# Zero-weight matmuls added into the open attention output bank while the planned recent TensorE use is low

## The chip, the cores and the metric

One core of one Trainium2 chip runs the whole program. The metric is the device time of one execution in microseconds (us); lower is better. The kernel before has a median of 971.56 us over 3 runs (968.69 to 973.88).

## The reference, cut to what matters

A pre-norm transformer block on 2048 rows of 640 numbers in bf16: attention with 32 heads of 20 columns, no mask, then a gated MLP of width 1728, each added to its input.

```python
def _A_ref(x, wqkv, wo):
    H = 32; Dh = D // H
    qkv = (x @ wqkv).reshape(B, S, 3, H, Dh)...
    scores = jnp.einsum("bhqd,bhkd->bhqk", q, k) * (Dh ** -0.5)
    p = _softmax(scores, axis=-1)
    o = jnp.einsum("bhqk,bhkd->bhqd", p, v)
    return o... @ wo
def _B_ref(x, w_gate, w_up, w_down):
    h = _gelu(x @ w_gate) * (x @ w_up)
    return h @ w_down
h = x + _A_ref(_layernorm(x), A_wqkv, A_wo)
h2 = h + _B_ref(_layernorm(h), B_w_gate, B_w_up, B_w_down)
```

The 32 x 2048 x 2048 exponentials of the softmax are the largest single item of work.

## The kernel before, in words

**Stages.** The first 40 us or so load x and the weights, do the first layer norm and project the first keys and queries. Then comes attention, in 7 chunks of queries (`CHUNKS`: 512, 512, 256, 256, 256, 128, 128). A chunk is cut into slots of 512 output columns (32 slots in all), a slot into 64 tiles of 128 keys x 512 score columns. What follows attention for a chunk (output projection, second layer norm, MLP: `post`, line 938) runs in the background of the next chunk's attention; for the last chunk it is the tail of the kernel.

**A unit of attention** (`unit`, line 787) is 3 tiles, then 2, in turn: banks 0 to 2 of PSUM and banks 3 and 4. TensorE writes the scores (`qk_mms`, line 804; recorded at L808) as up to 4 matmuls beside each other in row strips of 32. ScalarE takes the exponential of the whole unit in one instruction into a ring of 18 tiles (`pts` and `pts2`, which lies in `rege`). Some 8 tiles of a slot get their exponential on VectorE instead (`d_exp`, line 759, L768 and after), from a bank of the background (7 or 5). When two rows of 4 tiles ("quads") are done, one planned operation multiplies them with V (line 885): 4 matmuls of a quad beside each other in column strips of 32, accumulated in bank 6, 32 rows of it for each of 4 heads. It is called PV here; the ring's places come free when the whole operation has ended, since the semaphore goes with its last matmul. After a slot's last PV (`final`) VectorE copies bank 6 out (`osb`, line 904), and `epilogue` (line 899) transposes and divides; the next slot's first PV waits for that copy.

**The order of the work** is not left to the engines. Each operation is handed to a planner (`Sched.op`, line 52) with its engine, a duration, a priority (`P_QK` 0, `P_PV` 1, `P_EPI` 2, `P_BG` 3), what it reads and writes, the banks it takes, and `util`, the array time that it counts for. `Sched.schedule` (line 83) simulates the engines and, whenever one is free, gives it the ready operation of the best priority; on TensorE it prefers, below the first priority, an operation of the same mode (row strips, column strips, full array). `emit` (line 204) writes each engine's list in that order, with semaphore waits. An operation, once started, isn't interrupted.

**The filler that is there already** (lines 157 to 172): where TensorE is free in the plan and nothing is ready, and bank 7 has no owner, and the planned `util` of the last 3.4 us (`WARM_WIN`) is under half of that (`WARM_MIN`), a full 128x128 by 512 matmul of K data into bank 7 (`sc.warm`, line 1051) is planned, 0.215 us long. Nobody reads its result.

Of the kernel before, what the change touches and what calls it, by code (L numbers as in the profile page):

```python
# [15 lines left out]
SEM_ANY = 0.036  # L16
DRAIN = {"pe": 0.165, "act": 0.115, "dve": 0.085, "pool": 0.05, "sp": 0.0}
WARM_WIN, WARM_MIN = 3.4, 0.5
PE_AGE = 1.5

MODE_SWITCH = {"pe": 0.105, "act": 1.28}
# [19 lines left out]
class Sched:  # L41
# [3 lines left out]
    def __init__(self, nc):  # L45
        self.nc = nc
        self.ops = []
        self.lw = {}
        self.rd = {}
        self.warm = None  # L50

    def op(self, eng, fns, dur, prio, reads=(), writes=(), acq=(), rel=(), after=(), sem=None, lat=None, mode=None, util=0.0):
        o = Op()
# [29 lines left out]
    def schedule(self):  # L83
        ops = self.ops
        for o in ops:
            o.nd = len(o.deps)
            for d in o.deps:
                ops[d].succ.append(o.i)
        free_at = [0.0] * 8
        owner = [None] * 8  # L90
        last = [None] * 8
        ready = {e: [] for e in ENGINES}
        future = {e: [] for e in ENGINES}
        free = {e: 0.0 for e in ENGINES}
        mode = {e: None for e in ENGINES}
        for o in ops:
            if o.nd == 0:
                heapq.heappush(ready[o.eng], (o.prio, o.i))
        events = [0.0]
        done = 0  # L100
        order = []
        t = 0.0
        recent = collections.deque()
        total = len(ops)
        while done < total:
            assert events, "no operation can start"
            t = heapq.heappop(events)
            while events and events[0] <= t + 1e-9:
                heapq.heappop(events)
            for e in ENGINES:  # L110
                while future[e] and future[e][0][0] <= t + 1e-9:
                    _, p, i = heapq.heappop(future[e])
                    heapq.heappush(ready[e], (p, i))
                if free[e] > t + 1e-9:
                    continue
                skipped = []
                kept = set()
                chosen = None
                while ready[e]:
                    p, i = heapq.heappop(ready[e])  # L120
                    o = ops[i]
                    got = []
                    for bk in o.acq:
                        for b in bk.allowed:
                            if owner[b] is None and free_at[b] <= t + 1e-9 and b not in got and b not in kept:
                                got.append(b)
                                break
                        else:
                            got = None
                            break  # L130
                    if got is None:

                        if p[0] == 0:
                            kept.update(bk.allowed[0] for bk in o.acq)
                        skipped.append((p, i))
                        continue
                    skipped.append((p, i))
                    if chosen is None:
                        chosen, banks = o, got
                        if e != "pe" or p[0] < 1 or o.mode == mode[e] or t - o.ready > PE_AGE:  # L140
                            break
                    elif o.mode == mode[e]:
                        chosen, banks = o, got
                        break
                    if len(skipped) >= 60:
                        break
                for s in skipped:
                    if chosen is None or s[1] != chosen.i:
                        heapq.heappush(ready[e], s)
                if chosen is not None:  # L150
                    for bk, b in zip(chosen.acq, banks):
                        bk.b = b
                        owner[b] = bk
                        if last[b] is not None:
                            chosen.deps = set(chosen.deps)
                            chosen.deps.add(last[b])
                if chosen is None:
                    if e == "pe" and self.warm is not None:
                        while recent and recent[0][0] < t - WARM_WIN:
                            recent.popleft()  # L160
                        b = self.warm_bank
                        if owner[b] is None and free_at[b] <= t + 1e-9 and sum(x for _, x in recent) < WARM_MIN * WARM_WIN:
                            o = Op()
                            o.i, o.eng, o.fns, o.dur, o.lat = len(ops), "pe", [self.warm], 0.215, DRAIN["pe"]
                            o.prio, o.sem, o.tag, o.mode, o.util = (9, 0), None, "warm", "full", 0.213
                            o.deps = set(self.warm_deps) | ({last[b]} if last[b] is not None else set())
                            o.acq, o.rel, o.succ = [], [], []
                            if all(hasattr(ops[d], "fin") and ops[d].fin + 0.06 <= t for d in self.warm_deps):
                                ops.append(o)
                                last[b] = o.i  # L170
                                chosen = o
                                total += 1
                    if chosen is None:
                        continue
                o = chosen
                o.start = t
                if o.util:
                    recent.append((t, o.util))
                if o.mode is not None:
                    if mode[e] not in (None, o.mode):  # L180
                        o.dur += MODE_SWITCH[e]
                    mode[e] = o.mode
                free[e] = t + o.dur
                o.fin = t + o.dur + o.lat
                heapq.heappush(events, free[e])
                for bk in o.rel:
                    b = bk.b
                    owner[b] = None
                    free_at[b] = o.fin + SEM_LAT.get((e, "pe"), SEM_ANY)
                    last[b] = o.i  # L190
                    heapq.heappush(events, free_at[b])
                for s in o.succ:
                    q = ops[s]
                    q.ready = max(q.ready, free[e] if q.eng == e == "pe" else o.fin + SEM_LAT.get((e, q.eng), SEM_ANY))
                    q.nd -= 1
                    if q.nd == 0:
                        heapq.heappush(future[q.eng], (q.ready, q.prio, q.i))
                        heapq.heappush(events, q.ready)
                order.append(o)
                done += 1  # L200
        self.order = order
        self.span = max(o.fin for o in ops)
# [93 lines left out]
P_QK, P_PV, P_EPI, P_BG = 0, 1, 2, 3  # L296


def bass_sequential_preLN__mha_block__glu_gated_geglu__prompt_kernel(
# [12 lines left out]
    with ExitStack() as es:  # L312
        sc = Sched(nc)
        op = sc.op

        def sb(name, shape, dt=BF16):
            return es.enter_context(nc.sbuf_tensor(name, shape, dt))
# [15 lines left out]
        ident = sb("ident", [128, 128])  # L333
        identf = sb("identf", [128, 128], FP32)
        sel = sb("sel", [128, NA, H])
        sel0 = sb("sel0", [128, 4, 32])
        off0 = sb("off0", [128, 1], FP32)
        stats = sb("stats", [128, 4, 2, 6], FP32)
# [88 lines left out]
        def cst(fn, key, n=128):  # L427
            op(POOL, fn, 0.1 + n * 0.001, P_BG, writes=[key, "pool"])
# [6 lines left out]
        def fills(g0, g1, c0, c1):  # L435
# [3 lines left out]
            for c in range(c0, c1):  # L439
# [6 lines left out]
        cst(I("affine_select", out=sel[:], in_=sel[:], compare_op=ALU.is_ge, fill=0.0, base=DH - 1,  # L446
              pattern=[[-128, NA], [DH, H]], channel_multiplier=-1), "sel", 160)
        cst(I("memset", sel0[:], 0.0), "sel0")
        cst(I("memset", off0[:], 0.0), "off0", 1)
        for j in range(4):  # L450
            cst(I("memset", off0[32 * j:32 * j + 1, :], OFF), "off0", 1)
# [335 lines left out]
        def unit(u):  # L787
# [52 lines left out]
            while pv_wait:  # L840
# [35 lines left out]
                    acq = [bk]  # L876
                else:
                    bk, acq = pv_bank[s_], []
                fns, reads = [], ["vones"]
                for have in quads:  # L880
                    for kk in range(nk):
                        for pt, pkey, (_, g, kb, j) in have:
# [4 lines left out]
                                         tile_position=(0, 32 * j), skip_group_check=True))  # L887
                            pv_open.add((s_, j))
                            reads += [pkey, ("v", kt, g // 4)]
                op("pe", fns, 0.218 * len(quads), P_PV, mode="col", util=0.213 * len(quads), reads=reads, writes=[("O", s_), "pvseq"], acq=acq)  # L890
                if final:
                    assert not d_done and not d_raw
                    epilogue(s_, bk)

# [43 lines left out]
        def post(c, banks, tail):  # L938
# [88 lines left out]
            for tt in range(tb, tb + nt):  # L1027
                t = q0 // 128 + tt - tb
                i = t % 2
                for hf in range(2):  # L1030
# [19 lines left out]
        q_bound0(PRO, P_EPI)  # L1050
        sc.warm = I("matmul", PS[:, 512 * 7:512 * 8], kt_all[:, 0, 0:128], kt_all[:, 0, 0:512], start=True, stop=True,
                    skip_group_check=True)
        sc.warm_bank = 7
        sc.warm_deps = tuple(sc.lw[kk] for kk in k_keys[0][0])
        for kt in range(NT):
# [69 lines left out]
```

## Time and profile before

| | |
|---|---|
| median of 3 runs | 971.56 us |
| the profiled execution's own time | 969.62 us |
| its span, first to last instruction | 967.9 us |
| mean granted TensorE clock | 0.965 |
| ScalarE busy | 884.8 us (91%) |
| TensorE busy | 861.9 us (89%) |
| VectorE busy | 830.8 us (86%) |

A busy time is the union of the records of an engine's instructions. The end of a matmul is modelled, and records of consecutive instructions of one engine overlap, since an instruction begins while the one before it drains; so a busy engine need not be at its peak, and a wait shows shorter as idle time than it delays the next start.

### The profile page before, as it was taken

The page shows a single profiled execution, that of the slowest core. Times are in us where ns is not written, and L with a number is a line of the kernel's source. Part 1 is how long each engine was busy: PE and PEld are TensorE (multiplying, and loading weights), DVE is VectorE, ACT ScalarE, POOL GpSimd, SP SyncE. Part 2 cuts the span into 40 slices and gives each one's busy share as a digit, 9 for nine tenths or more (in the row PEclk, how much of TensorE's full clock was granted, in tenths as well). Part 3 has the DMA queues.
Part 4 walks back from the last instruction along what each step waited for, and adds up shares of the span by engine and source line. Part 5 has one row for each costly group of instructions (what it writes and reads, how often), then busy time and mean ns, then how long its engine had stood idle before and what let it go on. Part 6 is the DMA issues. An engine that isn't in the chain of part 4 may idle for free.

```text
span 967.9 us, 22233 instructions
## 1 busy us (share of the span) xinstructions
PE 861.9 (89%) x9668; PEld 366.4 (38%) x9668; DVE 830.8 (86%) x1804; ACT 884.8 (91%) x789; POOL 17.8 (2%) x25
## 2 busy tenths in 40 slices
PE   3999899998788899998888998999889999998998
PEld 1432222222132223233243333344334445655577
DVE  8758988998799898987899998798989899889953
ACT  4798999989999999999999999999989999998931
POOL 7000000000000000000000000000000000000000
PEclk9996998999999999999999899999979999998999
DMA  6220203227100000001000000001000000000000
GB/s 244 68 63 25 62 8 85 69 74 263 42 1 2 1 1 1 1 15 41 1 2 2 2 1 1 1 9 29 22 1 1 2 28 3 2 24 2 3 22 15
DMA packets 22041, 30.04 MB, mean 31 GB/s; under 512 B 1964, under 2 KB 19464, under 8 KB 21944
## 3 DMA queue, kind: packets, MB, share of 16 engines
q1 hardware_dynamic: 21944, 28.63, 9.2%
q8 instruction: 75, 1.23, 0.6%
q14 instruction: 22, 0.18, 0.1%
HBM read 20.12 MB, written 8.09 MB: 29 GB/s over the span
## 4 chain that ended last, share of the span: by engine, by line
ACT 70%; PE 20%; DVE 8%; issue 0%; DMA 0%; DVEq 0%
ACT pts L320 44%; ACT rege L320 24%; PE ps L808 5%; PE ps L571 4%; PE ps L320 4%; PE ps L984 3%; PE ps L1035 3%; DVE rege L320 3%; DVE rege L768 1%; ACT L320 1%; DVE qt_all L320 1%; PE ps L535 1%; DVE stats L320 1%; DMA rege<-in_A_x_dram 0%; DVE regw L601 0%
## 5 line engine op out<-in xcount | busy, mean ns | idle before, releaser
L320 ACT ACTIVATE pts<-ps 128x1536 bf16<-128x1536 f32 x480 | 569.9, 1338 | 26.5 <-PE ps L808 16.3
L808 PE MATMUL ps<-qt_all,kt_all 32*128 32x256 bf16 (+2 forms) x3584 | 315.0, 296 | 61.0 <-ACT pts L320 36.8
L320 ACT ACTIVATE rege<-ps 128x1536 bf16<-128x1536 f32 x239 | 295.6, 1339 | 6.1 <-PE ps L808 4.2
L808 PEld LDWEIGHTS ps<-qt_all,kt_all 32*128 32x128 bf16 x3584 | 98.3, 93 | 293.7 <-ACT pts L320 158.8
L320 DVE TENSOR_TENSOR qt_all<-qt_all 128x1024 bf16<-128x1024 bf16 (+1 forms) x240 | 164.7, 686 | 2.8
L984 PE MATMUL ps<-rege,regw 128*128 128x256 bf16 (+2 forms) x980 | 152.9, 292 | 6.3 <-ACT rege L320 2.5
L320 PE MATMUL ps<-pts,v_all 128*21 128x256 bf16 (+2 forms) x2098 | 144.9, 299 | 0.0
L768 DVE TENSOR_SCALAR rege<-ps 128x512 int16<-128x512 f32 x154 | 105.7, 687 | 43.8 <-PE ps L808 43.0
L320 PE MATMUL ps<-rege,v_all 128*21 128x256 bf16 (+2 forms) x1294 | 118.0, 301 | 0.5 <-DVE rege L320 0.5
L320 DVE TENSOR_SCALAR qt_all<-qt_all 128x1024 bf16<-128x1024 int16 (+1 forms) x288 | 116.0, 419 | 1.7
L984 PEld LDWEIGHTS ps<-rege,regw 128*128 128x128 bf16 x980 | 74.0, 98 | 61.5 <-issue 21.3
L571 PE MATMUL ps<-regw 128*128 128x320 bf16 (+1 forms) x360 | 88.9, 361 | 4.7 <-DVE rege L768 2.1
L1035 PE MATMUL ps<-regw,rege 128*128 128x320 bf16 x448 | 79.0, 304 | 2.3 <-DVE rege L1024 0.8
L768 DVE TENSOR_SCALAR qt_all<-ps 128x512 int16<-128x512 f32 x96 | 65.8, 687 | 5.0 <-PE ps L808 4.2
L320 DVE TENSOR_SCALAR rege<-rege 128x1024 int16<-128x1024 int16 (+2 forms) x166 | 67.8, 424 | 1.1
L320 DVE TENSOR_TENSOR rege<-rege 128x1024 bf16<-128x1024 bf16 (+3 forms) x103 | 66.3, 647 | 1.2
L320 PEld LDWEIGHTS ps<-pts,v_all 128*21 128x21 bf16 x2098 | 51.3, 92 | 39.6 <-issue 33.3
L320 PE MATMUL ps<-kt_all 128*128 128x512 bf16 x160 | 48.4, 395 | 6.8 <-DVE rege L768 5.2
L1035 PEld LDWEIGHTS ps<-regw,rege 128*128 128x128 bf16 x448 | 37.7, 98 | 33.5 <-issue 15.6
L320 PEld LDWEIGHTS ps<-rege,v_all 128*21 128x21 bf16 x1294 | 41.9, 93 | 21.9 <-issue 15.3
L571 PEld LDWEIGHTS ps<-regw 128*128 128x128 bf16 x360 | 29.3, 100 | 49.8 <-issue 19.6
L1024 DVE TENSOR_TENSOR rege<-rege,ps 128x512 bf16<-128x512 bf16 (+1 forms) x53 | 36.0, 680 | 14.0 <-PE ps L984 13.9
(83 smaller groups left out, 593.8 us busy)
## 6 DMA issues: line engine op xcount, KB each, us to landing
rege<-in_A_x_dram SPq DMA_DIRECT2D x6, 640.0 KB, 4.9
q_rows<-regw SPq DMA_DIRECT2D x20, 128.0 KB, 1.7
out_dram<-rege SPq DMA_DIRECT2D x16, 160.0 KB, 1.8
regw<-in_B_w_gate_dram SPq DMA_DIRECT2D x1, 2160.0 KB, 8.0
regw<-in_B_w_up_dram SPq DMA_DIRECT2D x1, 2160.0 KB, 14.0
regw<-in_B_w_down_dram SPq DMA_DIRECT2D x1, 2080.0 KB, 18.7
kt_all<-k_rows SPq DMA_DIRECT2D x12, 160.0 KB
qt_all<-q_rows SPq DMA_DIRECT2D x12, 160.0 KB
```

Source lines behind the costliest of these rows:

```text
L320: return lambda eng: getattr(eng, method)(*args, **kwargs)
L535: op("pe", lambda eng, a=a: eng.transpose(bank16(bk, D)[:, 128 * a:128 * a + 128], src[:, a * 128:(a + 1) * 128], ident[:]), 0.055, prio, ...
L571: yield op("pe", lambda eng, l=l, r=r, k=k: eng.matmul(bank(bk, n), l, r, start=(k == 0), stop=(k == len(steps) - 1)), c_mm(n), prio, mode ...
L768: d_ops.append(op("dve", lambda eng: eng.tensor_scalar(v[:, 512 * h:512 * h + 512], bank(b), EXP_MUL, -32000.0, ALU.mult, ALU.max), c_dve( ...
L808: return lambda eng: eng.matmul(out()[:, kk * nq:(kk + 1) * nq], kt_all[32 * j:32 * j + 32, g, kt * 128:(kt + 1) * 128], qt_all[32 * j:32 ...
L984: op("pe", lambda eng, a=a, f=f, fi=fi: eng.matmul(bank(bk)[:, fi * nq:(fi + 1) * nq], w[:, a, F0[f]:F0[f] + 128], hnT[:, a, 128 * tb:128 ...
L1024: hdone.append(op("dve", lambda eng, bu=bu, fv=fv, w=w: eng.tensor_tensor(fv, fv, bank(bu, w), ALU.mult), c_dve(w), p, reads=[ku, ("ha", k ...
L1035: op("pe", lambda eng, f=f, o=o, hf=hf, bk=bk: eng.matmul(bank(bk, 320), ha_f[:, o:o + 128], wd[:, f, hf * 320:(hf + 1) * 320], start=(f = ...
```

## The change

The planner keeps `live`: true from a PV that isn't its slot's last to the slot's last PV, so while bank 6 holds an open sum. There are two new places for filler, both made of a "pad": 4 matmuls in column strips of 32, with weights of zeros (`zer`, 128x32) and 512 columns of K, which add 0 to all of bank 6 (`start=False`).

- Where TensorE is free in the plan and the planned recent use is under the old limit, filler no longer needs bank 7: while `live`, a pad is planned when bank 7 is taken or the array is in column mode; otherwise the old matmul, as before.
- A PV that finds the planned use of the last 3.4 us, its own counted, under 0.42 of that gets pads inside its own operation, 0.215 us each, until the limit is reached or its own `util` is at least 1.1 (from 0.426 for two quads, so up to 4). Its semaphore then goes with the last pad.

Besides, one memset on GpSimd for `zer`, and two more things that a PV's reads are checked against.

```diff
--- before.py
+++ after.py
@@ -16,6 +16,7 @@
 SEM_ANY = 0.036
 DRAIN = {"pe": 0.165, "act": 0.115, "dve": 0.085, "pool": 0.05, "sp": 0.0}
 WARM_WIN, WARM_MIN = 3.4, 0.5
+PAD_WIN, PAD_MIN = 3.4, 0.42
 PE_AGE = 1.5
 
 MODE_SWITCH = {"pe": 0.105, "act": 1.28}
@@ -48,6 +49,8 @@
         self.lw = {}
         self.rd = {}
         self.warm = None
+        self.pad = None
+        self.final = set()
 
     def op(self, eng, fns, dur, prio, reads=(), writes=(), acq=(), rel=(), after=(), sem=None, lat=None, mode=None, util=0.0):
         o = Op()
@@ -101,6 +104,7 @@
         order = []
         t = 0.0
         recent = collections.deque()
+        live = False
         total = len(ops)
         while done < total:
             assert events, "no operation can start"
@@ -159,20 +163,35 @@
                         while recent and recent[0][0] < t - WARM_WIN:
                             recent.popleft()
                         b = self.warm_bank
-                        if owner[b] is None and free_at[b] <= t + 1e-9 and sum(x for _, x in recent) < WARM_MIN * WARM_WIN:
+                        free7 = (owner[b] is None and free_at[b] <= t + 1e-9
+                                 and all(hasattr(ops[d], "fin") and ops[d].fin + 0.06 <= t for d in self.warm_deps))
+                        if sum(x for _, x in recent) < WARM_MIN * WARM_WIN and (free7 or live):
                             o = Op()
-                            o.i, o.eng, o.fns, o.dur, o.lat = len(ops), "pe", [self.warm], 0.215, DRAIN["pe"]
-                            o.prio, o.sem, o.tag, o.mode, o.util = (9, 0), None, "warm", "full", 0.213
-                            o.deps = set(self.warm_deps) | ({last[b]} if last[b] is not None else set())
-                            o.acq, o.rel, o.succ = [], [], []
-                            if all(hasattr(ops[d], "fin") and ops[d].fin + 0.06 <= t for d in self.warm_deps):
-                                ops.append(o)
+                            o.i, o.eng, o.lat = len(ops), "pe", DRAIN["pe"]
+                            o.prio, o.sem, o.tag, o.util = (9, 0), None, "warm", 0.213
+                            o.acq, o.rel, o.succ, o.dur = [], [], [], 0.215
+                            if live and (mode[e] == "col" or not free7):
+                                o.fns, o.mode, o.deps = list(self.pad), "col", set()
+                            else:
+                                o.fns, o.mode = [self.warm], "full"
+                                o.deps = set(self.warm_deps) | ({last[b]} if last[b] is not None else set())
                                 last[b] = o.i
-                                chosen = o
-                                total += 1
+                            ops.append(o)
+                            chosen = o
+                            total += 1
                     if chosen is None:
                         continue
                 o = chosen
+                if e == "pe" and self.pad is not None and o.tag and o.tag[0] == "O":
+                    while recent and recent[0][0] < t - PAD_WIN:
+                        recent.popleft()
+                    u = sum(x for _, x in recent) + o.util
+                    while u < PAD_MIN * PAD_WIN and o.util < 1.1:
+                        o.fns = o.fns + self.pad
+                        o.dur += 0.215
+                        o.util += 0.213
+                        u += 0.213
+                    live = o.i not in self.final
                 o.start = t
                 if o.util:
                     recent.append((t, o.util))
@@ -333,6 +352,7 @@
         ident = sb("ident", [128, 128])
         identf = sb("identf", [128, 128], FP32)
         sel = sb("sel", [128, NA, H])
+        zer = sb("zer", [128, 32])
         sel0 = sb("sel0", [128, 4, 32])
         off0 = sb("off0", [128, 1], FP32)
         stats = sb("stats", [128, 4, 2, 6], FP32)
@@ -446,6 +466,7 @@
         cst(I("affine_select", out=sel[:], in_=sel[:], compare_op=ALU.is_ge, fill=0.0, base=DH - 1,
               pattern=[[-128, NA], [DH, H]], channel_multiplier=-1), "sel", 160)
         cst(I("memset", sel0[:], 0.0), "sel0")
+        cst(I("memset", zer[:], 0.0), "zer", 32)
         cst(I("memset", off0[:], 0.0), "off0", 1)
         for j in range(4):
             cst(I("memset", off0[32 * j:32 * j + 1, :], OFF), "off0", 1)
@@ -876,7 +897,7 @@
                     acq = [bk]
                 else:
                     bk, acq = pv_bank[s_], []
-                fns, reads = [], ["vones"]
+                fns, reads = [], ["vones", "zer"] + k_keys[0][0]
                 for have in quads:
                     for kk in range(nk):
                         for pt, pkey, (_, g, kb, j) in have:
@@ -887,8 +908,9 @@
                                          tile_position=(0, 32 * j), skip_group_check=True))
                             pv_open.add((s_, j))
                             reads += [pkey, ("v", kt, g // 4)]
-                op("pe", fns, 0.218 * len(quads), P_PV, mode="col", util=0.213 * len(quads), reads=reads, writes=[("O", s_), "pvseq"], acq=acq)
+                pv = op("pe", fns, 0.218 * len(quads), P_PV, mode="col", util=0.213 * len(quads), reads=reads, writes=[("O", s_), "pvseq"], acq=acq)
                 if final:
+                    sc.final.add(pv)
                     assert not d_done and not d_raw
                     epilogue(s_, bk)
 
@@ -1050,6 +1072,8 @@
         q_bound0(PRO, P_EPI)
         sc.warm = I("matmul", PS[:, 512 * 7:512 * 8], kt_all[:, 0, 0:128], kt_all[:, 0, 0:512], start=True, stop=True,
                     skip_group_check=True)
+        sc.pad = [I("matmul", PS[32 * j:32 * j + 32, 512 * 6:512 * 7], zer[:], kt_all[:, 0, 0:512], start=False, stop=False,
+                    tile_position=(0, 32 * j), skip_group_check=True) for j in range(4)]
         sc.warm_bank = 7
         sc.warm_deps = tuple(sc.lw[kk] for kk in k_keys[0][0])
         for kt in range(NT):
```

## Rows read from the trace of the kernel before

**Rows 1.** The page's first part: busy time of each engine, share, instructions.
```profile
PE 861.9 (89%) x9668; PEld 366.4 (38%) x9668; DVE 830.8 (86%) x1804; ACT 884.8 (91%) x789; POOL 17.8 (2%) x25
```
**Rows 2.** The page's fourth part: the chain that ended last, by engine, by line.
```profile
ACT 70%; PE 20%; DVE 8%; issue 0%; DMA 0%; DVEq 0%
ACT pts L320 44%; ACT rege L320 24%; PE ps L808 5%; PE ps L571 4%; PE ps L320 4%; PE ps L984 3%; PE ps L1035 3%; DVE rege L320 3%; DVE rege L768 1%; ACT L320 1%; DVE qt_all L320 1%; PE ps L535 1%; DVE stats L320 1%; DMA rege<-in_A_x_dram 0%; DVE regw L601 0%
```
**Rows 3.** The page's second part: granted clock in tenths, in 40 equal slices.
```profile
PEclk9996998999999999999999899999979999998999
```
**Rows 4.** Windows of the ten half-clock stretches: length, busy by engine, clock.
```profile
core 0: us, PE busy (x) PEld busy (x) DVE busy (x) ACT busy (x) POOL busy (x), PEclk, DMA share, GB/s
77.20:94.30 17.10, 16.50 (x83) 3.84 (x81) 12.96 (x26) 13.07 (x12) 0.00 (x0) 0.50 0.06 16
...
708.70:718.90 10.20, 9.74 (x84) 4.29 (x84) 8.41 (x20) 7.60 (x7) 0.00 (x0) 0.50 0.01 2
...
821.30:824.70 3.40, 3.13 (x19) 1.75 (x15) 3.40 (x9) 3.39 (x3) 0.00 (x0) 0.50 0.00 0
...
sum 68.30, PE 65.51 PEld 21.81 DVE 56.43 ACT 55.19 POOL 0.00; mean PE 6.55 PEld 2.18 DVE 5.64 ACT 5.52 POOL 0.00
```
**Rows 5.** ScalarE's waits over the whole span: total us, times, longest.
```profile
ACT pts L320 <- PE ps L808: 16.3, 21, 4.1
...
ACT pts L320 <- PE ps L320: 9.7, 7, 2.5
...
ACT rege L320 <- PE ps L808: 4.2, 8, 1.2
ACT rege L320 <- PE ps L320: 1.6, 1, 1.6
```
**Rows 6.** Groups by line and shape: the exponentials of 3 and 2 tiles.
```profile
L320 ACT ACTIVATE pts<-ps 128x1536 bf16<-128x1536 f32 x240 | 371.9, 1549 | 17.7 <-PE ps L808 14.1 <-PE ps L320 3.2
L320 ACT ACTIVATE pts<-ps 128x1024 bf16<-128x1024 f32 x240 | 270.2, 1126 | 8.8 <-PE ps L320 6.5 <-PE ps L808 2.2
```
**Rows 7.** The chain in order of time: start, us, engine, instructions merged.
```profile
463.80 4.52 ACT pts L320 x4
470.58 4.52 ACT pts L320 x4
```
**Rows 8.** Windows of the 3.4 us ahead of each fall of the clock.
```profile
323.00:326.40 3.40, 1.95 (x22) 0.59 (x21) 3.40 (x8) 3.40 (x4) 0.00 (x0) 1.00 0.00 0
538.00:541.40 3.40, 2.54 (x37) 1.10 (x37) 3.40 (x9) 3.40 (x4) 0.00 (x0) 1.00 0.00 0
...
817.90:821.30 3.40, 2.69 (x81) 1.84 (x75) 3.40 (x7) 3.38 (x4) 0.00 (x0) 1.00 0.02 5
...
sum 34.00, PE 22.85 PEld 9.22 DVE 33.78 ACT 33.88 POOL 0.62; mean PE 2.29 PEld 0.92 DVE 3.38 ACT 3.39 POOL 0.06
```
**Rows 9.** The old filler: its group, its count from 230.8 to 326.4, that window.
```profile
L320 PE MATMUL ps<-kt_all 128*128 128x512 bf16 x160 | 48.4, 395 | 6.8 <-DVE rege L768 5.2 <-DVE qt_all L768 1.4
L320 PE MATMUL ps<-kt_all 128*128 128x512 bf16 x53 | 15.9, 387 | 2.2 <-DVE rege L768 2.2
230.80:326.40 95.60, 77.47 (x630) 24.07 (x630) 83.63 (x189) 95.04 (x85) 0.00 (x0) 1.00 0.15 59
```
**Rows 10.** Timeline of TensorE around one PV of two quads, full clock.
```profile
94.89 0.39 PE L320 MATMUL ps<-pts,v_all 128*21 128x512 bf16 x3
...
95.12 0.38 PE L320 MATMUL ps<-pts,v_all 128*21 128x512 bf16 x1
...
95.44 0.58 PE L571 MATMUL ps<-regw 128*128 128x320 bf16 x3
```
**Rows 11.** Timeline around a slot's last PV, a long one.
```profile
694.30 0.29 PE L320 MATMUL ps<-pts,v_all 128*21 128x256 bf16 x3
...
695.28 0.40 PE L808 MATMUL ps<-qt_all,kt_all 32*128 32x256 bf16 x6
695.40 2.36 ACT L320 ACTIVATE pts<-ps 128x1536 bf16<-128x1536 f32 x2 [0.88 <-PE ps L320]
```
**Rows 12.** Timeline of GpSimd: a memset like the new one, and its last work.
```profile
4.08 0.20 POOL L320 MEMSET sel<- 128x128 bf16 x1
...
11.94 7.18 POOL L320 MEMSET qt_all<- 128x1792 f32 x4
```

## The prediction, made before the changed kernel was run

> **What bounds the kernel now.** I read the page's totals first. ScalarE is busy 884.8 us, TensorE 861.9, VectorE 830.8 [rows 1]: three engines near the end of their room, so totals don't settle it. The chain of waits does: 70% of the span runs over ScalarE, 44% and 24% of it in the exponentials into the two parts of the ring, and 20% over TensorE [rows 2]. The chain in order of time shows what a quiet stretch looks like: from 463.80 to 470.58 there are three pairs of exponentials, 6.78 us or 2.26 us a pair [rows 7], with nothing between them. There the time is ScalarE's, and no matmul made faster can help.
>
> So a gain has to come from where ScalarE waits. Its waits for the scores are 16.3 and 4.2 us (29 times); its waits for PV, which has to free a place in the ring, are 9.7 and 1.6 us (8 times) [rows 5]. Next I read the clock. It is full in most slices, with dips to 6, 7 or 8 tenths in single ones [rows 3]. Cut at its changes, there are ten stretches at half clock between 77 and 887 us (of the two levels 2.4 and 1.2 GHz the second), together 68.3 us; ScalarE is busy in 55.19 of them and idle in 13.1 [rows 4]. TensorE is busy 65.51 of the 68.3 there: at half clock it is the bound. That is where the chance lies.
>
> **The size of the chance.** A wait delays the next exponential by more than the idle time shown, as the records overlap: a pair's records last 1549 + 1126 ns [rows 6] but a pair takes 2.26 us [rows 7], so 0.21 us of each lies under the next. I take 20 of the 29 waits for scores to lie in the ten stretches, by their share of the idle time (13.1 of 20.5 us). Lost there: 13.1 + 20 x 0.21 = 17.3 us, or 0.25 us for each us at half clock. It is uneven: the stretch from 77.2 has 4.0 idle of 17.1, that from 821.3 has none [rows 4].
>
> **What precedes a fall, and whether the change reaches it.** In the 3.4 us ahead of the ten falls ScalarE runs through (33.88 of 34.0) but TensorE is busy 22.85 of 34, from 1.95 to 2.69 of 3.4 in the rows shown [rows 8]. So 1.1 us a time is idle, and more of the busy part is drain and narrow score strips. The existing filler could have stood there; it needs bank 7, which epilogues, background chains and VectorE's tiles also hold, and it was used 160 times in all, 53 of these between 230.8 and 326.4 [rows 9], in which the clock never fell until the end. New filler goes into bank 6 and needs no other bank: 1.1 us holds five pads of 0.22. Nine of the ten falls lie well inside an open slot by the order of the work; the one at 159.1 comes just after a slot's end, when `live` is off. I let two falls stay, or new ones come, of 6.8 us each: 13.7 x 0.25 = 3.4 us. Gain: 17.3 - 3.4 = 13.9 us.
>
> **What a pad costs on TensorE.** No row shows a pad, but a PV quad is the same shape but for 21 weight columns instead of 32: two quads start at 94.89 and 95.12 and the next operation at 95.44 [rows 10], so 0.23 us a quad and some 0.3 with the change of mode. I take 0.22 to 0.23 us a pad; the ends are 0.21 (512 columns at 2.4 GHz) and 0.33.
>
> Here a rule of the Trainium skill speaks against the change ("TensorE: Matmul & The Clock Gate", the section Part 3 on packing small matmuls): weight loads run beside matmuls in flight only when their row group differs, and a pad's four loads use all rows. With that page's P / 1.2 for a load of 32 columns, an estimate by it is 0.11 us more a pad, and some 3 us more in the sum. The trace disagrees: eight loads of full height cost the two quads of [rows 10] 0.02 us each at most.
>
> **Pads where the plan is idle.** TensorE is idle 967.9 - 861.9 = 106 us [rows 1], some 20 of these at both ends, so at most 390 pads fit; I take half, 200, since the limit stops them. The nearest row for their price is the old filler: 53 of them in 95.6 us in which ScalarE was idle 0.56 us, all causes counted [rows 9]: at most 0.011 us each, so 2.2 us. Below, 0; above, if each held up a score matmul on the path, 200 x 0.22 = 44 us, which that row excludes by far. What hides them is the double buffer: TensorE writes one unit's scores while ScalarE works 0.9 or 1.3 us on the other. If that cover is gone (both banks waiting), a pad costs its whole length.
>
> **Pads inside PV.** These can't be split: next scores queue behind up to 4 x 0.22 = 0.9 us more, and so does the release of the ring's places that ScalarE waits for. They are needed where TensorE was never free but did work that counts little, as at slot ends with their transposes: I estimate 50 PVs (32 slots, one or two each) with two pads, 22 us of TensorE. Their nearest row is a long PV, 694.30 to 695.28, after which an exponential had waited 0.88 us [rows 11]. There are 8 such waits for 32 slot ends [rows 5], one in four; pads mostly stand elsewhere in the slot, so I take one in eight: 50 x 0.44 / 8 = 2.8 us. Ends: 0 and 22.
>
> **The rest.** `zer` is a memset like that of `sel0`, at most 0.20 us; GpSimd goes on until 19.1 us [rows 12], and attention begins after 40, so nothing; if that cover were gone, 0.2 us. PV's two new reads are of K data that the scores of the same slot already waited for, and of `zer`: nothing. No DMA is added or moved. VectorE's and the background's work may start a pad later, 0.2 us, beside ScalarE's work; VectorE's slot copy is late next if a last PV is padded. The planner orders everything anew, so other waits (8 for PV, 11.3 us [rows 5]) shift by some 3 us either way: in the range, not in the sum.
>
> **The sum.** 969.62 - 13.9 + 2.2 + 2.8 = 960.7 us for an execution like the profiled one. That one is 1.9 us under the median of the runs shown, so against 971.56 I forecast **962.7 us**, 0.9% faster.
>
> **Rivals.**
>
> *Pads free, clock full* (0.15): all ten falls gone and the double buffer hides everything, as it hides the old filler [rows 9]. 971.6 - 17.3 = 954.3 us. Against it: falls at slot ends, where no sum is open.
>
> *The pads don't hold the clock* (0.15): zero weights in narrow strips may do less than full K data, or the plan's times drift from the chip's, so that pads stand in the wrong 3.4 us. Everything lost at half clock stays, plus the 2.2 to 5 us of price: 974 to 976.5 us, take 974.5. For it: no pad has run in this trace. Against it: PV and pads have nearly the same shape, and between 230.8 and 326.4, where little but attention and filler ran, the clock stayed full [rows 9].
>
> *PV with pads becomes the wait* (0.12), the other side: the place is the score matmul behind a padded PV. A score matmul has 0.9 to 1.3 us less its own 0.4 [rows 11] to be in time; an unpadded PV takes 0.55, a padded one with two to four pads 1.0 to 1.4, which no longer fits into the shorter half. With 100 padded PVs of four pads, 88 us, and one in four landing, 22 us: 971.6 - 13.9 + 2.2 + 22 = 982 us. It decides from a landed price of 13.9 - 2.2 + 4.9 = 16.6 us on. For it, [rows 11]; against it, the planner knows the length when it orders, and idle pads come first, so that PV seldom finds the limit unmet.
>
> **How the numbers follow.** A measurement of this kernel tells about 0.5%, 4.9 us, from no change: under 966.7 is faster, over 976.4 slower. The forecast has 0.58; its own range, with the two unknown prices and 3 us of reordering, is 956 to 970, of which some 0.85 is faster. Faster: 0.58 x 0.85 + 0.15 = 0.64. Same: 0.09 + 0.12 of the second rival = 0.21. Slower: 0.12 + 0.03 = 0.15. The range that leaves 0.2 out runs from the first rival's time less a little to the second rival's: 952 to 976.
>
> **What would show it right or wrong.** Right: fewer than four half-clock stretches between 77 and 887 us and a mean clock over 0.985; ScalarE's waits for scores from 20.5 to about 10 us; a new group of matmuls of 32 columns by `zer`, 800 to 1500 records; the pair still 2.26 us. Wrong: stretches at half clock as before (second rival), or full clock but more waits of ScalarE for L808 or PV than before (third). If `zer` has few records, the change doesn't do what it says.

## The result, and the profile after

The changed kernel takes 946.2 us (median of 4 runs, 945.62 to 946.83) against 972.72 us of the kernel before (4 runs, 968.69 to 975.69): a ratio of 0.973, 95% interval 0.9692 to 0.9768. The profiled execution took 945.62 us, its span is 943.9. I had forecast 962.7 us, in a range of 952 to 976: the sign was right, the size was not. One execution of all that follow, at the limit 0.35, was in the chip's slower state and is left out.

The page of the changed kernel: busy times, then the granted clock in 40 slices (to be held against [rows 1, 3]).

```profile
PE 852.4 (90%) x10332; PEld 367.6 (39%) x10388; DVE 829.6 (88%) x1804; ACT 881.4 (93%) x789; POOL 17.9 (2%) x26
...
PEclk9999999999999999999999999999999999999999
```

No slice is below full speed. By its weight loads TensorE has 720 more matmuls than before (10388 and 9668). Its busy time can't be held against the old one, since 56 matmul records are missing here (10332 for 10388 loads). Three of the ten old half-clock stretches, by the same times, in windows (columns as in [rows 4]):

```profile
77.20:94.30 17.10, 16.67 (x139) 5.23 (x137) 16.87 (x36) 17.10 (x16) 0.00 (x0) 1.00 0.05 16
541.40:548.30 6.90, 6.30 (x86) 2.56 (x81) 6.23 (x14) 6.90 (x8) 0.00 (x0) 1.00 0.01 2
708.70:718.90 10.20, 9.80 (x142) 4.82 (x142) 10.12 (x22) 10.20 (x11) 0.00 (x0) 1.00 0.01 2
```

ScalarE, idle 4.0 us in the first of them before, has no idle time left in any of the three. How that comes about is seen in the timeline ahead of 77.2, where the first fall had come (start, length, engine, line, operation, count):

```profile
76.06 0.33 PE L936 MATMUL ps<-identf,osb 128*128 128x128 f32 x1
76.31 0.34 PEld L339 LDWEIGHTS ps<-kt_all,zer 128*32 128x32 bf16 x12
76.32 0.83 PE L339 MATMUL ps<-kt_all,zer 128*32 128x512 bf16 x12
...
77.08 0.39 PE L829 MATMUL ps<-qt_all,kt_all 32*128 32x512 bf16 x3
```

Between an epilogue's transpose and the next scores, where TensorE had been idle for 0.69 us before, stand three pads. They start 0.22 us behind each other (0.83 less the 0.39 of one matmul's record, for two steps), so a pad costs what a PV quad does. The Trainium skill ("TensorE: Matmul & The Clock Gate", the section Part 3 on packing small matmuls) has loads that share their row group wait for the matmul in flight; twelve loads of full height here fit into 0.34 us beside the matmuls, so the measurement decides against the 0.11 us more a pad that I had worked out from that page. The group of the pads, and what is left of the old filler (160 in [rows 9]; the program now holds 56, of which 43 are recorded):

```profile
L339 PE MATMUL ps<-kt_all,zer 128*32 128x512 bf16 x824 | 70.6, 384 | 0.1
L339 PE MATMUL ps<-kt_all 128*128 128x512 bf16 x43 | 13.2, 383 | 1.1 <-issue 0.8 <-DVE qt_all L339 0.3
```

The program holds 206 pads of four matmuls: 197 in idle places and only 9 inside PVs, in 6 of 256. ScalarE's waits (us in total, times, longest), beside [rows 5]:

```profile
ACT pts L339 <- PE ps L829: 5.1, 5, 4.1
ACT pts L339 <- PE ps L339: 3.0, 4, 1.7
...
ACT rege L339 <- PE ps L339: 1.6, 1, 1.6
```

The waits for scores fell from 20.5 to 5.1 us; 4.1 of these are the first one of attention, which was there before. That is the clock: 26 of the 29 old waits lie in the half-clock stretches or end within 1 us behind one. But the waits for PV also fell, from 11.3 to 4.6, and this I had not foreseen. The attention stretch got 24.6 us shorter (883.2 to 858.6, first to last exponential), with the start (41.2 and 41.4) and the tail (43.5 and 43.9) nearly as before.

### The profile page after: what moved, and what is told of

The parts are those of the page before. It is cut to its first block, busy times and chain, and to the rows that moved or that the text cites. A ratio compares the mean times of both kernels' runs of the same rounds, so it can differ in the third digit from the quotient of the medians.

```text
span 943.9 us, 23617 instructions
## 1 busy us (share of the span) xinstructions
PE 852.4 (90%) x10332; PEld 367.6 (39%) x10388; DVE 829.6 (88%) x1804; ACT 881.4 (93%) x789; POOL 17.9 (2%) x26
## 3 DMA queue, kind: packets, MB, share of 16 engines
q8 instruction: 81, 1.33, 0.6%
## 4 chain that ended last, share of the span: by engine, by line
ACT 70%; PE 17%; DVE 12%; issue 0%; DMA 0%; DVEq 0%
ACT pts L339 45%; ACT rege L339 24%; PE ps L592 4%; DVE rege L339 4%; PE ps L1006 4%; PE ps L829 3%; PE ps L339 2%; PE ps L1057 2%; DVE rege L789 2%; DVE qt_all L339 2%; ACT L339 1%; DVE regw L622 1%; DVE stats L339 1%; PE ps L556 1%; DMA rege<-in_A_x_dram 0%
## 5 line engine op out<-in xcount | busy, mean ns | idle before, releaser
L829 PE MATMUL ps<-qt_all,kt_all 32*128 32x256 bf16 (+2 forms) x3584 | 304.0, 289 | 47.4 <-ACT pts L339 29.2
L339 ACT ACTIVATE rege<-ps 128x1536 bf16<-128x1536 f32 x239 | 298.9, 1369 | 1.7 <-PE ps L339 1.6
L829 PEld LDWEIGHTS ps<-qt_all,kt_all 32*128 32x128 bf16 x3584 | 96.0, 92 | 274.6 <-ACT pts L339 161.4
L1006 PE MATMUL ps<-rege,regw 128*128 128x256 bf16 (+2 forms) x955 | 146.4, 287 | 12.8 <-ACT rege L339 4.8
L339 PE MATMUL ps<-pts,v_all 128*21 128x256 bf16 (+2 forms) x2098 | 138.8, 290 | 0.9 <-DVE rege L339 0.5
L339 PE MATMUL ps<-rege,v_all 128*21 128x256 bf16 (+2 forms) x1294 | 113.3, 292 | 0.0
L592 PE MATMUL ps<-regw 128*128 128x320 bf16 (+1 forms) x342 | 81.5, 348 | 3.5 <-ACT regw L562 0.8
L339 PE MATMUL ps<-kt_all,zer 128*32 128x512 bf16 x824 | 70.6, 384 | 0.1
## 6 DMA issues: line engine op xcount, KB each, us to landing
regw<-in_B_w_up_dram SPq DMA_DIRECT2D x1, 2160.0 KB, 15.4
```

What stands on the lines that cost most here:

```text
L339: return lambda eng: getattr(eng, method)(*args, **kwargs)
L592: yield op("pe", lambda eng, l=l, r=r, k=k: eng.matmul(bank(bk, n), l, r, start=(k == 0), stop=(k == len(steps) - 1)), c_mm(n), prio, mode ...
L829: return lambda eng: eng.matmul(out()[:, kk * nq:(kk + 1) * nq], kt_all[32 * j:32 * j + 32, g, kt * 128:(kt + 1) * 128], qt_all[32 * j:32 ...
L1006: op("pe", lambda eng, a=a, f=f, fi=fi: eng.matmul(bank(bk)[:, fi * nq:(fi + 1) * nq], w[:, a, F0[f]:F0[f] + 128], hnT[:, a, 128 * tb:128 ...
```

## The experiments

**A measure for what follows.** Besides the waits I use ScalarE's lost time: how much later than undisturbed (1.33 us after one of three tiles, 0.90 after one of two) the next instruction starts. It counts the delays hidden in the overlap of records too. A delay counts to a half-clock stretch if the instruction ahead of it starts in the stretch or up to 1 us before it. Before the change the lost time is 21.4 us in the stretches and 23.0 outside them; after it, 0 and 18.4. All of it is read from one execution of each kernel. The figures of 31 and 26 us in the first expectations counted gaps behind table loads too, 8 us in either kernel.

**Which of the two places?** Idle places alone:

```diff
-                    while u < PAD_MIN * PAD_WIN and o.util < 1.1:
+                    while False:
```

> Only the pads in the plan's idle places (218 of them, 54 full matmuls); none inside a PV. Theory A (the pads in idle places hold the clock, those inside PV hardly matter: the plan has 9 of them in 6 of 256 PVs): clock at least 0.995, 944 to 950 us. Rival B (the PV pads close the one stretch that idle places can't reach): two or more stretches at half clock return, 952 to 960 us.

Measured: 949.01 us (948.01 to 950.45), ratio 0.9766 (0.974 to 0.9792), clock 1.0 in the profiled execution and 0.996 to 0.998 in the others. Theory A. The 2.8 us more lie behind attention: its last exponential ends at 899.5 us, that of the changed kernel at 899.9, but from there to the end it takes 46.8 us instead of 44.0.

Pads inside PV alone:

```diff
-                        if sum(x for _, x in recent) < WARM_MIN * WARM_WIN and (free7 or live):
+                        if sum(x for _, x in recent) < WARM_MIN * WARM_WIN and free7:
...
-                            if live and (mode[e] == "col" or not free7):
+                            if False:
```

> Only the pads inside PV (now 40 planned); in idle places the old full matmul, and only with bank 7 free (127 planned). Theory A: half the falls stay, 4 to 7 stretches at half clock, 958 to 968 us. Rival B: at most 2 stretches, 946 to 952 us.

Measured: 965.36 us, ratio 0.9927 (0.9895 to 0.9959), 13 stretches at half clock, 61.4 us in sum. The time is in theory A's range, the falls are more than it allowed. The pads in idle places do the work.

**Order or pads?** The new planning moves everything. First the new order with no pad in the program:

```diff
         sc.schedule()
+        sc.order = [o for o in sc.order if not (o.tag == "warm" and o.mode == "col")]
+        for o in sc.order:
+            o.fns = [f for f in o.fns if f not in sc.pad]
```

> The changed kernel's order of all other work, with every pad left out of the program (56 full matmuls stay). Theory A (the gain is the clock's, and the waits that went at full clock were its after-effects): as many or more falls than before the change, clock 0.95 to 0.97, 966 to 985 us. Rival C (the new order is worth some 5 us by itself, since ScalarE lost 31 us outside the half-clock stretches before and 26 us after): 960 to 967 us with ten falls.

Measured: 980.09 us, ratio 1.0065 (1.0039 to 1.0091). Its clock:

```profile
PEclk9996979989596899999688789899999999999999
```

It is at half clock for 163.8 us in 18 stretches and loses 40.1 us in them: with the pads gone, and 56 full matmuls where the kernel before has 160, the clock falls more often than before the change. So the pads themselves hold it. But the lost time outside these stretches is 15.4 us, in 732 us of attention at full clock. That is the rate of the changed kernel (18.4 in 859) and under that of the kernel before (23.0 in 815): the order's share doesn't need the clock. That speaks for rival C beside theory A, and the next run weighs it: the old order, with pads put into the gaps of its plan (the helper that walks TensorE's list is shortened here).

```diff
         sc.schedule()
+        for o in sc.order:
+            if o.eng == "pe":
+                while live and o.start - t >= GAP:
...
+                    if sum(x for _, x in recent) >= WARM_MIN * WARM_WIN:
+                        break
+                    p.fns, p.deps = list(sc.pad), set()
+                    order.append(p)
+                    t += 0.215
```

> The old kernel's order, instruction by instruction, with 71 pads put into gaps of at least 0.32 us of its plan for TensorE while a slot is open and the planned use is low (160 full matmuls stay). Theory A: at most 3 falls, clock at least 0.985, 945 to 953 us; ScalarE's lost time outside half clock also falls from 31 to about 26 us. Rival C: the falls go but 5 us of the gain stay away, 951 to 957 us, with the waits of before at full clock (2.5 us of ScalarE for PV near 211 us) still there.

Measured: 954.76 us (952.28 to 954.99), ratio 0.9819 (0.9791 to 0.9846), clock 0.995 with two stretches left, at 45 and 683 us, 5.4 us lost in them. ScalarE's waits:

```profile
ACT pts L323 <- PE ps L323: 11.0, 7, 2.5
ACT pts L323 <- PE ps L813: 5.3, 2, 4.1
ACT rege L323 <- PE ps L323: 1.6, 1, 1.6
ACT rege L323 <- PE ps L813: 1.6, 2, 1.4
```

The waits for scores are 6.9 us, nearly as few as in the changed kernel; those for PV are 12.6 us, as before the change, the one of 2.5 us included, and the lost time outside falls is 22.9. This is rival C: 71 pads give 15.1 us of the 24.0 in span without moving anything. Of the 8.9 us left, up to 5.4 are the two stretches that stay; outside them the lost time is 4.5 us above the changed kernel's, and that is the order's, less what the changed kernel pays for its 135 pads more.

**What do pads cost?** More of them in the idle places of the old order:

```diff
-GAP = 0.32
+GAP = 0.24
+FILL_MIN = 0.8
```

(`FILL_MIN` takes the place of `WARM_MIN` where pads are put in.)

> The old order once more, with 306 pads instead of 71 in its gaps (limit 0.8 of the last 3.4 us, gaps from 0.24 us). Theory A (idle pads are free): clock at least 0.995, 947 to 951 us, and ScalarE's lost time outside falls stays at 22 to 24 us, the old order's own. Rival D (a pad in a gap costs 0.011 us or more, as the prediction had it): 2.6 us or more over that for 235 more pads, from 952 us on.

Measured: 955.44 us (953.1 to 961.51), ratio 0.9832 (0.9789 to 0.9876), clock 0.998. The lost time outside falls is 27.3 us, 4.3 more than with 71 pads; some 1 us of that is a wait for PV that lay inside a fall there. (4.3 - 1) / 235 = 0.014 us a pad: rival D, and near the 0.011 of the prediction. It is an estimate from one execution of each; the times alone (955.44 and 954.76 us) don't tell the two kernels apart. By it idle pads are cheap, not free.

One pad more behind every PV of the changed kernel, nothing else moved:

```diff
         sc.schedule()
+        for o in sc.order:
+            if o.eng == "pe" and o.tag and o.tag[0] == "O":
+                o.fns = o.fns + sc.pad
```

> The changed kernel's order with one pad more in every one of the 256 PVs, placed after planning, so that nothing else moves: 256 x 0.22 = 56 us more of TensorE. Theory A (a PV pad is hidden by the double buffer unless the scores are late, one in eight as the prediction had it): 7 us more, 950 to 956 us. Theory E (nothing lands): 945 to 948 us. Third rival of the prediction (one in four or more lands): from 960 us on.

Measured: 968.47 us (967.33 to 969.89), ratio 0.9961 (0.9944 to 0.9979), clock 0.998.

```profile
ACT pts L339 <- PE ps L829: 10.5, 23, 4.1
ACT pts L339 <- PE ps L339: 3.8, 4, 1.7
...
ACT rege L339 <- PE ps L829: 2.0, 4, 1.3
```

22.3 us more than the changed kernel for 256 pads is 0.087 us each, 40% of their length: the third rival's price and more. (A short fall cost 1.5 us in the profiled execution; five of the ten have a clock of 1.0.) By the lost time nearly all of it lies in waits for scores: 27 that show idle time where there were 5, and many shorter than the records' overlap, which show none.

**Place or limit?** The old filler alone with a higher limit:

```diff
-WARM_WIN, WARM_MIN = 3.4, 0.5
+WARM_WIN, WARM_MIN = 3.4, 0.8
```

> The kernel before, only with the limit of its old filler raised from 0.5 to 0.8: 234 full matmuls planned instead of 160, still only with bank 7 free. Theory A (what kept the clock from holding is the place, not the limit): 6 or more falls stay, 962 to 973 us. Rival F (more filler of any kind is enough): at most 3 falls, 950 to 958 us.

Measured: 977.27 us, ratio 1.0029 (1.0001 to 1.0058).

```profile
PEclk9996989999999899999999999989989999998999
```

With 234 full matmuls instead of 160 there are still 12 falls. The old filler stands only where bank 7 is free, and 71 pads that need no bank, in the old order, left two: it is the place. The time is even above theory A's range.

The same constant in the changed kernel, at 0.6:

> The changed kernel with the limit of idle filler at 0.6 instead of 0.5: 275 idle pads, 87 full matmuls, 9 pads in PVs. Theory A: the clock is full already, so only the order can change: 943 to 951 us.

Measured: 947.05 us (945.73 to 948.01), ratio 0.9738 (0.9705 to 0.9772), one short fall: no better than 0.5. At 0.45 and 0.35:

> The changed kernel with the limit of idle filler at 0.45 instead of 0.5: 157 idle pads, 62 full matmuls, 16 pads in PVs. If the limit has room to spare: clock at least 0.995, 945 to 951 us. If 0.5 is just enough: 2 to 5 falls, 949 to 957 us. On the order: if the shorter waits for PV at slot ends are a property of planning with idle pads, ScalarE waits for PV under 6 us again; if they are chance, 6 to 13 us.

> The same with the limit at 0.35: 86 idle pads, 40 full matmuls, 20 pads in PVs. If the limit sets how often the clock falls: 4 to 8 falls, 955 to 968 us. If the mere ability to place a pad with bank 7 taken is what counts, 0 to 3 falls and 946 to 954 us. On the order: as for the limit 0.45.

Measured: 947.94 us (947.67 to 948.32), clock 0.996, with two falls, and 960.18 us (955.89 to 970.21), ratio 0.988 (0.9846 to 0.9914), with nine. At 0.45 time and clock are those expected if there is room to spare, and only the two falls speak for the other case; at 0.35 the clock falls nearly as often as before the change. So the limit does set how often it falls, once a pad can be placed. The waits for PV were 7.1 us in both. By the bounds that I had set (under 6 us for a property of planning with idle pads) that is chance, though it is well under the 10.6 and more of the plans without them.

**Why the waits for PV got shorter.** They are 10.6 to 11.5 us in the three plans without idle pads (the kernel before, pads inside PV alone, the old filler at 0.8) and 3.1 to 7.1 in the five with them. A pad is of column mode, and so is PV; below the first priority the planner puts an operation off in favour of a later one of the array's present mode (line 140, for up to 1.5 us). So a pad may make PV go at once where a full-array filler let background work pass it. To test this, pads that leave the mode alone:

```diff
-                                o.fns, o.mode, o.deps = list(self.pad), "col", set()
+                                o.fns, o.mode, o.deps = list(self.pad), None, set()
```

> The changed kernel, but a pad in an idle place leaves the planner's record of the array's mode as it was, so that it no longer makes the planner prefer column work next (197 idle pads, 99 full matmuls). If that preference is what shortens the waits for PV at slot ends: ScalarE waits 10 us or more for PV, as in the three plans without idle pads (10.6 to 11.5 us), 950 to 955 us at full clock. If not: 3 to 7 us of such waits, as in the plans with them, and 944 to 950 us.

Measured: 953.74 us (951.53 to 954.91), ratio 0.9802 (0.976 to 0.9844), clock 1.0.

```profile
ACT pts L339 <- PE ps L339: 11.7, 9, 2.2
...
ACT pts L339 <- PE ps L829: 4.3, 2, 4.1
...
ACT rege L339 <- PE ps L339: 2.3, 2, 1.5
```

The waits for PV are back, 14.0 us, at full clock and with 197 idle pads again (in other places, and with 99 full matmuls for 56). Then, on top of it, PV may no longer be put off:

```diff
-                        if e != "pe" or p[0] < 1 or o.mode == mode[e] or t - o.ready > PE_AGE:
+                        if e != "pe" or p[0] < 2 or o.mode == mode[e] or t - o.ready > PE_AGE:
```

> The kernel of the run before (pads leave the mode as it was), and the planner may no longer put a ready PV off in favour of a background operation in the array's present mode (182 idle pads, 86 full matmuls). If that putting off is how the mode matters: ScalarE's waits for PV are back at 3 to 7 us, from 14.0, and 944 to 950 us. If the mode works in another way: 10 us or more of them, 950 to 957 us.

Measured: 949.34 us (947.87 to 949.85), ratio 0.9755 (0.9691 to 0.982), clock 1.0.

```profile
ACT pts L339 <- PE ps L339: 5.3, 5, 2.3
...
ACT rege L339 <- PE ps L339: 1.5, 1, 1.5
```

6.8 us instead of 14.0: where PV is never put off, its waits are shorter. How far this is the way in which a pad's mode works can be read from the plans that the kernels make, each wait of ScalarE matched with the PV that it follows. In the three plans without idle pads 8 to 11 PVs are put off, which start 5.7 to 7.7 us later in all than when they were first passed over, and 6.1 to 8.1 us of waits come behind them. In the five with idle pads it is 4 to 9 PVs and 3.0 to 5.2 us, with 1.6 to 4.2 us of waits. So 5.7 of the 6.7 us that the change saved come behind PVs put off (8.1 before, 2.4 after). But pads that leave the mode alone don't bring these back: with 8 PVs put off, by 6.0 us, only 4.1 of the 14.0 us come behind them. Of the 9.4 us between that run and the changed kernel the putting off is 1.7; the rest comes behind PVs that weren't put off, and its cause stays open. The kernel before with PV never put off, and no pad, was not tried. What separates this kernel's 949.3 us from the 946.2 of the change was not tried; every plan differs from the next by a few us. No version tried beats the changed kernel.

## Why the prediction was wrong, point by point

- **The bound and the mechanism** were right: ScalarE sets the pace, TensorE is the bound only at half clock, and filler that needs no bank of its own keeps the clock up. The old order with pads shows it without anything else moved.
- **The size of the chance** was a term too small: 17.3 us, where 21.4 were lost. I counted the idle time inside the stretches, 13.1 us. Waits that end up to 1 us behind a stretch hold another 2.9, and delays shorter than the overlap, which show no idle time, 1.4. The overlap itself came out right by luck: 20 waits of 0.21 us were taken, and it was 26 of 0.16. Missing: 4.1 us.
- **Falls that stay**, 3.4 us: none stayed, not even the one at 159.1, just after a slot's end.
- **Pads where the plan is idle**: 200 estimated, 197 in the program; 0.011 us estimated, 0.014 from the run with more of them. That is 2.8 us instead of 2.2: this term holds.
- **Pads inside PV**: 100 estimated, 9 in the program, since idle pads come first (I had this as an argument against the third rival, and not in the count). Their price was too low the other way: one in eight, measured 40%. 9 x 0.087 = 0.8 us instead of 2.8. With my count at the measured price, the change would have paid 8.7 us.
- **"The planner orders everything anew, so other waits (8 for PV) shift by some 3 us either way"** is the step that failed most: left out of the sum as a shift of either sign. The waits for PV shifted one way, by 6.7 us, and in each of the five plans with idle pads of column mode they are shorter than in any of the three without. I had priced the pads' time on TensorE, not what a pad does to the planner's next choices. 5.7 of the 6.7 us came behind PVs that the planner puts off. That the pad's mode brings this about isn't shown: pads that leave the mode alone gave 14.0 us of waits, most of them behind PVs that weren't put off.
- **The sum.** 4.1 + 3.4 + 2.0 + 6.7 - 0.6 = 15.6 us, where 15.1 lie between the 960.7 us forecast for the profiled execution and its 945.62 (16.5 between 962.7 and the median of 946.2). Some terms are lost time and some idle time, so the sum needn't close better. The range ended at 952 because each of these was taken as uncertain alone; all four went the same way.
- **Rivals.** "Pads free, clock full" was nearest, at 954.3 us, short by the order and the size of the chance. "Pads don't hold the clock" fell with the first profile. "PV with pads becomes the wait" is true of a pad in PV, and does not occur as the program has only 9.

## What to carry to other kernels

Where an engine's pace depends on what it did before, look for filler that can go into a resource already open (here a sum to which zeros are added), and put it where the engine itself is idle: behind each PV, ahead of the scores that another engine waits for, the same filler cost about six times as much (0.087 and 0.014 us). When a list is planned, a filler is also an operation to the planner: what it leaves behind (here the mode) changes the choices after it, and that has to be read as part of the change, in the plan itself. Delays of a pipelined engine are read from the spacing of starts, not from idle time alone.

## What had not been expected of the hardware

Matmuls with weights of zeros in four strips of 32 columns kept the granted clock at 1.0 for the whole of attention (4 runs), 206 times four of them beside 56 full filler matmuls. 71 times four, in the old order with its 160 full ones, took the mean clock from 0.965 to 0.995. In the new order without them, and with the 56 alone, it was 0.917.
